# Long convolution and gated MLP on one core: stage-1 and last-stage tasks split into halves of one PSUM pair, with a new hand-written order

## The chip, the core and the metric

The kernel runs on one core of a Trainium2 chip. The core has a matrix engine (PE, with its weight loads shown apart as PEld), a vector engine (DVE), a scalar engine (ACT), a small general engine (POOL) and a queue engine (SP) that issues DMAs. They run at the same time and wait for one another through semaphores. The metric is the device time of one execution in microseconds (us); lower is better. Matmuls write into PSUM, eight banks of 128 x 512 fp32; only DVE and ACT read it.

## The reference

Input x (2048 x 512, called A_q) is layer-normalised to xn. Branch A shifts k by a 4-tap filter, multiplies it by v and convolves the product along the sequence with a filter of length 2048 per channel, by FFT. Branch B is a gated MLP on xn with 1792 hidden columns. The result joins them:

```python
kv = k_shift * v
y  = irfft(rfft(pad(kv)) * rfft(pad(ssm_k)))[:S] + kv * ssm_D
s  = xn * y
h  = gelu(xn @ w_gate) * (xn @ w_up)
out = x + s * silu(h @ w_down)
```

All inputs and the output are bf16.

## The kernel before

**Branch A** replaces the FFT by a transform in two stages each way. In stage 1 the matrix F1 multiplies the filter's transposed rows (HTr; eight tasks called H0 to H7) and the product of k and v (V; eight tasks K0 to K7). A contraction is over 64 rows, so PE works as two 64-row tiles, and two matmuls run at once on the two halves of the partitions. One task is four matmuls of 512 columns and fills two PSUM pairs (a pair is two banks, 1024 columns). ACT or DVE copies each pair to SBUF (AST), for H an addition on DVE follows, and a DMA stores the result to a scratch tensor in HBM (ZH, ZK). Stage 2 loads it back and multiplies 32 x 32 tiles, 16 matmuls at once (L1029); the products of the spectra are taken on DVE; the inverse's first stage is again 32 x 32 tiles, goes through scratch ZI, and the inverse's last stage multiplies G1 in two 64-column tiles (L1274): eight results psy0 to psy7, one PSUM pair each, taken two to a task of eight matmuls.

**Branch B** goes over four groups of 512 rows. For each of 14 column blocks, `unit` makes a gate and an up product (four full-array matmuls each, L641), ACT takes the GELU out of PSUM (L1195) and DVE multiplies (L1204) into HT. `down` multiplies HT by Wd, 14 matmuls in three tasks (4, 5, 5) for each 128 rows.

**Layer norm** of the first rows: DVE's statistics (L848), a variance on ACT or DVE (L858, L859), a power on POOL (L861), the normalised tile (L870), four transposes on PE (L891), and a copy from PSUM to xnT (L632, L635).

**Start.** DVE zeroes a block (L696), and PE multiplies zeros twelve times to warm up. POOL makes index tables (two for F1, L671 and L672, and four for the other tables, L675 to L678). DVE multiplies the first two (L720), and the sines of ACT make F1 and the 32 x 32 tables. `m_turn` (four ACT operations, L753) prepares the inverse's tables, which two transposing DMAs bring into place.

**Order.** Each piece of work is a task. `SEQ` is a list, written out by hand, of all task numbers; a "b" takes the second of two engines a task may run on, DVE in place of ACT for most copies. The tasks are emitted in that order, so it fixes the order on every engine and queue: SP issues the loads and most stores, ACT issues the stores of ZH and ZI. Semaphore waits follow from the data, the SBUF slots and the PSUM banks. Slots and banks are given out while the list is walked: `Pool_.find` takes the one that a table of durations in the kernel says is free the longest. Gate, up and down products may hold four banks at a time (`NF_BANKS`); the pairs of branch A come from the same eight.

A run of neighbouring PE tasks that leave the full array for tiles, and return, is called an excursion below. Before, each stage-1 task and each last-stage task is an excursion by itself.

Of the kernel before, what the change touches and what calls it, by code (L numbers as in the profile page):

```python
# [413 lines left out]
def build_kernel(nc, A_q, A_k, A_v, A_shift_k, A_ssm_k, A_ssm_D, B_w_gate, B_w_up, B_w_down, out):  # L414
    with ExitStack() as es0:
# [524 lines left out]
        def stage1(x, u, Z):  # L940
# [3 lines left out]
            if x == "K":  # L944
                def halves(e):
                    for i in range(2):
                        for b in range(2):
                            k = slice(64 * b, 64 * b + 64)
                            trk.op("PE", lambda h, i=i, b=b, k=k: h.matmul(ps(psl(pp[i]), b), lhsT=F1[k, :], rhs=V[k, 2 * u + i, :], start=True, stop=True, tile_position=(64 * b, 0)),  # L949
                                   r=[R_F1, R_V[2 * u + i]], w=[R_ps[psl(pp[i])][b]], accum=True)  # L950
                s1_tasks[x].append(S.add([("PE", 2 * T_FWD)], halves, r=[bF1, bKV[u // 2]], w=pp, lat=150.0, mode=2))
            if x == "H":
# [8 lines left out]
                def rows(p):  # L961
                    return ps(psl(p)).rearrange("p (d r) -> p r d", r=2)
# [295 lines left out]
        for j in range(8):  # L1258
# [6 lines left out]
            if j % 2 == 0:  # L1265
                continue
# [94 lines left out]
```

## Time and profile before

| | us |
|---|---|
| runs: median of three | 192.35 |
| runs: lowest, highest | 191.08, 192.36 |
| the profiled execution | 191.04 |
| its span, first to last instruction | 189.24 |
| PE busy | 184.5 |
| DVE busy | 168.6 |
| ACT busy | 138.3 |

A line of the profile's timeline gives start, duration, engine, source line, operation, the tile written and the tile read, shapes, and the count of instructions merged; in brackets follows the idle time before it and who ended it. Names that end in q are an engine's queue, where it issues DMAs. Matmuls overlap in the array, so starts, not ends, tell their pace. A shape 64*128 is a 64-row tile, 128*64 a 64-column tile, 32*32 a small one.

### The profile page before, as it was taken

Reading aid. Unit: us, or ns where it says so; the run is one execution under the profiler, and the core shown is the slowest. Engines: PE = TensorE matmul, PEld = TensorE weight load, DVE = VectorE, ACT = ScalarE, POOL = GpSimd, SP = SyncE. Lnnn points to the kernel's source line nnn. Section 1 sums busy time; section 2 is a strip of 40 time slices with the busy share of each in tenths; the row PEclk is TensorE's granted clock in tenths of the full one; section 3 lists DMA queues with packets and bytes.
Section 4 is the critical chain, followed back from the end, with each engine's and each line's share of the span. In section 5 each row is a group of like instructions: output and inputs, shape, how many; then the busy total and the mean of one; then the engine's idle time right before and its main releaser. Section 6 shows DMA issues by size and latency. Waiting matters only on the chain.

```text
span 189.2 us, 3611 instructions
## 1 busy us (share of the span) xinstructions
PE 184.5 (97%) x1418; PEld 79.6 (42%) x1418; DVE 168.6 (89%) x255; ACT 138.3 (73%) x191; POOL 11.1 (6%) x26
## 2 busy tenths in 40 slices
PE   7899999999999999999999999999999999999993
PEld 2685453333333333334444434333433344444342
DVE  5889999999999999988699999999999955458974
ACT  3789897988688786997548869688997672254671
POOL 5312600000000000022000000000000000000000
PEclk9999999999999999999999999999999999999999
DMA  5999999998769994468998966778742435946644
GB/s 173 329 384 344 345 373 367 400 416 326 210 254 249 362 227 161 171 215 229 324 261 214 321 221 182 291 259 276 273 156 74 149 128 157 366 143 182 256 178 166
DMA packets 36422, 47.84 MB, mean 253 GB/s; under 512 B 7347, under 2 KB 26039, under 8 KB 36406
## 3 DMA queue, kind: packets, MB, share of 16 engines
q1 hardware_dynamic: 29878, 39.23, 64.2%
q10 hardware_dynamic: 6528, 8.39, 12.6%
q8 instruction: 11, 0.18, 0.4%
q14 instruction: 5, 0.04, 0.1%
HBM read 27.39 MB, written 14.68 MB: 222 GB/s over the span
## 4 chain that ended last, share of the span: by engine, by line
PE 97%; DVE 1%; ACT 0%; issue 0%
PE psall L641 82%; PE psall L1029 6%; PE psall L957 2%; PE psall L949 2%; PE psall L915 2%; PE psall L1274 2%; PE psall L891 1%; DVE G L1239 0%; DVE G L1238 0%; ACT G L1236 0%; DVE xnT L635 0%; DVE AST L696 0%; DVE COLS L695 0%
## 5 line engine op out<-in xcount | busy, mean ns | idle before, releaser
L641 PE MATMUL psall<-xnT,Wu 128*128 128x512 bf16 (+1 forms) x248 | 56.3, 359 | 0.0
L641 PE MATMUL psall<-xnT,Wg 128*128 128x512 bf16 (+1 forms) x248 | 55.8, 359 | 0.5 <-DVE xnT L635 0.5
L641 PE MATMUL psall<-Wd,HT 128*128 128x512 bf16 (+2 forms) x238 | 52.3, 367 | 0.0
L1195 ACT ACTIVATE GE<-psall 128x512 bf16<-128x512 f32 x54 | 31.6, 602 | 12.2 <-PE psall L641 10.9
L641 PEld LDWEIGHTS psall<-Wd,HT 128*128 128x128 bf16 x238 | 21.7, 98 | 27.6 <-issue 4.8
L641 PEld LDWEIGHTS psall<-xnT,Wu 128*128 128x128 bf16 x248 | 22.0, 98 | 26.4 <-issue 2.6
L641 PEld LDWEIGHTS psall<-xnT,Wg 128*128 128x128 bf16 x248 | 21.5, 98 | 27.4 <-issue 3.3
L1204 DVE TENSOR_TENSOR HT<-psall,GE 128x512 bf16<-128x512 f32 x43 | 28.8, 682 | 3.0 <-PE psall L641 2.9
L632 ACT ACTIVATE BO<-psall 128x1024 bf16<-128x1024 f32 x20 | 20.0, 1026 | 7.9 <-PE psall L1274 6.0
L1132 DVE TENSOR_TENSOR HSW<-KB,HSW 128x2048 bf16<-128x2048 bf16 x16 | 19.1, 1216 | 0.1
L632 ACT ACTIVATE HSW<-psall 128x1024 bf16<-128x1024 f32 x15 | 14.7, 1026 | 4.7 <-PE psall L1029 4.6
L632 ACT ACTIVATE KB<-psall 128x1024 bf16<-128x1024 f32 x13 | 13.2, 1039 | 2.4 <-PE psall L1029 2.4
L1012 DVE TENSOR_TENSOR KAC<-KAC,KTM 128x2048 bf16<-128x2048 bf16 x12 | 14.6, 1217 | 0.1
L1010 DVE TENSOR_TENSOR KTM<-KK,SKB 128x2048 bf16<-128x2048 bf16 x12 | 14.6, 1216 | 0.0
L632 ACT ACTIVATE AST<-psall 128x1024 bf16<-128x1024 f32 x12 | 12.3, 1026 | 2.4 <-PE psall L641 2.0
L1228 ACT ACTIVATE G<-psall 128x512 bf16<-128x512 f32 x12 | 7.1, 601 | 7.3 <-PE psall L641 7.3
L632 ACT ACTIVATE XN<-psall 128x1024 bf16<-128x1024 f32 x10 | 10.3, 1029 | 0.8 <-PE psall L957 0.8
L1230 DVE SCALAR_TENSOR_TENSOR G<-G,psall 128x512 bf16<-128x512 bf16 x12 | 7.8, 679 | 3.2 <-ACT G L1228 3.2
L848 DVE BATCH_NORM_STATS2 stats<-X 128x6 f32<-128x512 bf16 x16 | 10.6, 676 | 0.0
L861 POOL TENSOR_TENSOR mv<-mv,NHALF 128x1 f32<-128x1 f32 (+1 forms) x7 | 5.5, 784 | 76.4 <-DVE mv L859 71.9
L1132 DVE TENSOR_TENSOR KB<-KB,HSW 128x2048 bf16<-128x2048 bf16 x8 | 9.6, 1216 | 0.0
L1155 DVE TENSOR_TENSOR HSW<-HSW 128x2048 bf16<-128x2048 bf16 x8 | 9.6, 1215 | 0.0
(89 smaller groups left out, 165.8 us busy)
## 6 DMA issues: line engine op xcount, KB each, us to landing
BH<-ZH SPq DMA_DIRECT2D x8, 512.0 KB, 4.8
BK<-ZK SPq DMA_DIRECT2D x8, 512.0 KB, 5.3
HSW<-HSW SPq DMA_DIRECT2D x16, 256.0 KB, 4.1
ZI<-BO ACTq DMA_DIRECT2D x16, 256.0 KB, 3.1
BI<-ZI SPq DMA_DIRECT2D x8, 512.0 KB, 4.9
ZK<-AST SPq DMA_DIRECT2D x6, 512.0 KB, 3.3
ZH<-XN ACTq DMA_DIRECT2D x5, 512.0 KB, 3.3
Hn<-in_A_ssm_k_dram SPq DMA_DIRECT2D x4, 512.0 KB, 7.3
```

Source lines behind the costliest of these rows:

```text
L632: return h.activation(o, i, ACTF.Copy, scale=scale)
L641: return h.matmul(o, lhsT=l, rhs=r, start=st, stop=sp)
L848: t_stats[t] = op([("DVE", 670.0)], lambda e, h, t=t: h.bn_stats(stats[:, t, :], X[:, t, :]), r=[bX[q][t % 4]], w=[bst[t]], rr=[R_X[t]], w ...
L1010: op([("DVE", dur)], lambda e, h, j=j, m=m: h.tensor_tensor(KTM[:, m.slot, :, :], kk(j), sk(j), ALU.mult), r=need + [bSKB[j], a], w=[m], r ...
L1012: op([("DVE", dur)], lambda e, h, m=m: h.tensor_tensor(KAC[:, a.slot, :, :], KAC[:, a.slot, :, :], KTM[:, m.slot, :, :], ALU.add), r=[m], ...
L1029: trk.op("PE", lambda h: h.matmul(ps(s, i)[b, :], lhsT=wt(col)[a, :], rhs=data(col)[a, :], start=n < 16, stop=n >= len(todo) - 16, tile_po ...
L1132: return hd.tensor_tensor(pair(KB, *(2 * DM * z for z in slots())) if to else x, k, x, ALU.mult)
L1155: return hd.tensor_tensor(x, x, y, ALU.add)
L1195: op([("ACT", act(512))], lambda e, h: h.activation(GE[:, g.slot, :], bank(pg), ACTF.Gelu_apprx_tanh), r=[pg], w=[g], rr=lambda: R_bank(pg ...
L1204: op([("DVE", dve(512, 1))], lambda e, h: h.tensor_tensor(HT[:, q % 2, m, :], bank(pu), GE[:, g.slot, :], ALU.mult), r=[pu, g], w=[bHT[q][m]],
L1228: op([("ACT", act(n))], lambda e, h, g=g, pc=pc: h.activation(g, pc(), ACTF.Tanh, scale=0.5), r=[p], w=[bt], rr=lambda p=p: R_bank(p), ww= ...
L1230: op([("DVE", dve(512, 1))], lambda e, h, g=g, pc=pc: h.scalar_tensor_tensor(out=g, in0=g, scalar=1.0, in1=pc(), op0=ALU.add, op1=ALU.mult ...
```

## The change

Stage-1 tasks are split. Before, one task filled two pairs; for H each 512-column half of the input was spread over both pairs, one partition half to each. Now there are two tasks for each of H0 to H7 and K0 to K7; task i takes the i-th half of the columns (H) or the i-th row block (K), and writes one pair, a partition half to each of its two banks. For H the copy of pair i, 1024 elements as before, fills half of the columns in each of AST's four rows (runs of 256), where it filled two whole rows, and task i waits only for the transposed blocks of its own columns. The last stage's four tasks of two results become eight of one. There are 816 tasks in place of 796, and as many instructions on PE.

The list is new throughout. In it up to three of the new tasks stand side by side:

```text
before  stage 1: 16 excursions of one task (four matmuls)
        last:     4 excursions of one task (eight matmuls)
after   stage 1: 13 excursions, of 1 to 3 tasks (two matmuls each)
          H3_0 H2_0 H1_0 | H7_0 H1_1 H2_1 | H3_1 | H5_0 H7_1 | H5_1 H6_1 H6_0
          H4_0 H0_0 H0_1 | H4_1 K1_0 K1_1 | K0_1 K0_0 K3_0 | K3_1 K2_0 K2_1
          K5_1 K5_0 | K4_1 K4_0 | K7_0 K7_1 | K6_0 K6_1
        last:     3 excursions, of 2 or 3 tasks (four matmuls each)
          psy2 psy0 | psy4 psy3 psy1 | psy7 psy5 psy6
```

At the start, POOL now makes the two index tables for F1 ahead of the other four, and DVE multiplies them ahead of the zeros. ACT takes the sines, and with them a table load, ahead of the first two variances. `m_turn` moves from the first GELUs to behind the copies of H6. Both late loads of x come ahead of the stage-2 loads of ZH on SP.

```diff
-    "3 16 0 1 17 18 2 7 19 20 21 22 23 24 25 26 4 27 10 8 11 67 68 28 65 5 9 66 73 29 6 48 49 30 76b 77 78 87 12 74 75 69 91 86 90b 361 70 349 350 31 "
+    "2 16 17 18 19 20 21 7 0 22 10 23 24 25 3 4 5 26 6 8 11 9 12 27 28 29 1 65 66 67 68 73b 74 75 76b 77 78 48 86 90 49 30 87 91 31 69 70 79 80 32 "
...
             if x == "K":
-                def halves(e):
-                    for i in range(2):
+                for i in range(2):
+                    def halves(e, i=i):
                         for b in range(2):
                             k = slice(64 * b, 64 * b + 64)
...
-                s1_tasks[x].append(S.add([("PE", 2 * T_FWD)], halves, r=[bF1, bKV[u // 2]], w=pp, lat=150.0, mode=2))
+                    s1_tasks[x].append(S.add([("PE", T_FWD)], halves, r=[bF1, bKV[u // 2]], w=[pp[i]], lat=150.0, mode=2))
             if x == "H":
-                def pairs(e):
-                    for i in range(2):
+                bl = B(f"low{u}")
+                for i in range(2):
+                    def pairs(e, i=i):
                         for b in range(2):
                             k = slice(64 * b, 64 * b + 64)
-                            trk.op("PE", lambda h, i=i, b=b, k=k: h.matmul(ps(psl(pp[b]), i), lhsT=F1[k, :], rhs=HTr[k, u, 512 * i:512 * i + 512], start=True, stop=True, tile_position=(64 * b, 0)),
+                            trk.op("PE", lambda h, b=b, k=k: h.matmul(ps(psl(pp[i]), b), lhsT=F1[k, :], rhs=HTr[k, u, 512 * i:512 * i + 512], start=True, stop=True, tile_position=(64 * b, 0)),
...
+                    s1_tasks[x].append(S.add([("PE", T_FWD)], pairs, r=[bF1] + [bHTr[k][u // 4] for k in range(2 * i, 2 * i + 2)] + ([bFold] if u == 0 else []), w=[pp[i]], lat=150.0, mode=2))
+                for i in range(2):
+                    op(EV(1024), lambda e, h, i=i: copy(e, h, ast[x][a.slot][:, :, :, 256 * i:256 * i + 256], ps(psl(pp[i])).rearrange("p (b d r) -> p b r d", b=2, r=2)), r=[pp[i]], w=[a, bl],
...
-                op(EV(1024), lambda e, h: copy(e, h, ast[x][a.slot][:, 0, :, :], rows(pp[0])), r=[pp[0]], w=[a, bl], rr=lambda: R_ps[psl(pp[0])], ww=lambda: [R_AST[x][a.slot]])
-                op(EV(1024), lambda e, h: copy(e, h, ast[x][a.slot][:, 1, :, :], rows(pp[1])), r=[pp[1]], w=[a, bl], rr=lambda: R_ps[psl(pp[1])], ww=lambda: [R_AST[x][a.slot]])
...
-            if j % 2 == 0:
-                continue

             def y(e, j=j):
-                for jj in (j - 1, j):
-                    s, slot = psl(p_y[jj]), b_bi[jj].slot
-                    for i in range(2):
-                        for b in range(2):
...
-            S.add([("PE", 4 * T_FWD)], y, r=[bG1, *b_bi[j - 1:j + 1]], w=p_y[j - 1:j + 1], lat=150.0, mode=3)
+            S.add([("PE", 2 * T_FWD)], y, r=[bG1, b_bi[j]], w=[p_y[j]], lat=150.0, mode=3)
```

More of the change, by code (lines that the diff above doesn't have):

```diff
@@ L944, in stage1 @@
             if x == "K":
-                def halves(e):
-                    for i in range(2):
+                for i in range(2):
+                    def halves(e, i=i):
                         for b in range(2):
                             k = slice(64 * b, 64 * b + 64)
-                            trk.op("PE", lambda h, i=i, b=b, k=k: h.matmul(ps(psl(pp[i]), b), lhsT=F1[k, :], rhs=V[k, 2 * u + i, :], start=True, stop=True, tile_position=(64 * b, 0)),
+                            trk.op("PE", lambda h, b=b, k=k: h.matmul(ps(psl(pp[i]), b), lhsT=F1[k, :], rhs=V[k, 2 * u + i, :], start=True, stop=True, tile_position=(64 * b, 0)),
@@ L955, in pairs @@
                         for b in range(2):
                             k = slice(64 * b, 64 * b + 64)
-                            trk.op("PE", lambda h, i=i, b=b, k=k: h.matmul(ps(psl(pp[b]), i), lhsT=F1[k, :], rhs=HTr[k, u, 512 * i:512 * i + 512], start=True, stop=True, tile_position=(64 * b, 0)),
-                                   r=[R_F1, *R_HTr[u][2 * i:2 * i + 2]], w=[R_ps[psl(pp[b])][i]], accum=True)
-                s1_tasks[x].append(S.add([("PE", 2 * T_FWD)], pairs, r=[bF1] + [bHTr[k][u // 4] for k in range(KD)] + ([bFold] if u == 0 else []), w=pp, lat=150.0, mode=2))
@@ L961, in rows @@
[L961 to L965 removed]
+                            trk.op("PE", lambda h, b=b, k=k: h.matmul(ps(psl(pp[i]), b), lhsT=F1[k, :], rhs=HTr[k, u, 512 * i:512 * i + 512], start=True, stop=True, tile_position=(64 * b, 0)),
+                                   r=[R_F1, *R_HTr[u][2 * i:2 * i + 2]], w=[R_ps[psl(pp[i])][b]], accum=True)
@@ L1264, in build_kernel @@
             S.add([("SP", ISSUE)], ld, r=bZ["I"], w=[bi], nbytes=W_BI)
-            if j % 2 == 0:
-                continue
             def y(e, j=j):
-                for jj in (j - 1, j):
-                    s, slot = psl(p_y[jj]), b_bi[jj].slot
-                    for i in range(2):
-                        for b in range(2):
-                            c = slice(64 * b, 64 * b + 64)
-                            trk.op("PE", lambda h, i=i, b=b, c=c, s=s, slot=slot: h.matmul(ps(s, i)[c, :], lhsT=G1[:, c], rhs=BI[:, slot, 2 * b + i, :], start=True, stop=True, tile_position=(0, 64 * b)),
-                                   r=[R_G1, R_BI[slot]], w=[R_ps[s][i]], accum=True)
-            S.add([("PE", 4 * T_FWD)], y, r=[bG1, *b_bi[j - 1:j + 1]], w=p_y[j - 1:j + 1], lat=150.0, mode=3)
+                s, slot = psl(p_y[j]), b_bi[j].slot
+                for i in range(2):
+                    for b in range(2):
+                        c = slice(64 * b, 64 * b + 64)
+                        trk.op("PE", lambda h, i=i, b=b, c=c, s=s, slot=slot: h.matmul(ps(s, i)[c, :], lhsT=G1[:, c], rhs=BI[:, slot, 2 * b + i, :], start=True, stop=True, tile_position=(0, 64 * b)),
+                               r=[R_G1, R_BI[slot]], w=[R_ps[s][i]], accum=True)
+            S.add([("PE", 2 * T_FWD)], y, r=[bG1, b_bi[j]], w=[p_y[j]], lat=150.0, mode=3)
         for j in range(8):
```

2 lines of the change are left out of this document (1 added, 1 removed), and 43 rows, old and new, of the table SEQ.

## The prediction

> **What bounds the kernel now.** I read the page first, then the list of waits of PE, then the busy time by stage.
>
> ```profile
> span 189.2 us, 3611 instructions
> PE 184.5 (97%) x1418; PEld 79.6 (42%) x1418; DVE 168.6 (89%) x255; ACT 138.3 (73%) x191; POOL 11.1 (6%) x26
> PE 97%; DVE 1%; ACT 0%; issue 0%
> ```
> ```profile
> PE psall L641 <- DVE AST L696: 1.2, 1, 1.2
> PE psall L641 <- DVE xnT L635: 0.5, 1, 0.5
> ```
> ```profile
> 9.00:45.00 36.00, 36.00 (x247) 18.62 (x244) 34.97 (x59) 32.47 (x50) 5.03 (x7) 1.00 1.04 371
> 45.00:80.00 35.00, 35.00 (x173) 13.38 (x172) 34.79 (x45) 27.47 (x37) 0.00 (x0) 1.00 0.77 244
> ```
>
> The chain of waits is PE for 97% of the span, and the only waits that PE shows are 1.2 us at the start (for the zeros that the warm-up multiplies) and 0.5 us (for the first transposed xn). In the columns of the two stages (window, length, PE, PE weight loads, DVE, ACT, POOL, clock, DMA, GB/s) PE is busy all 71 us, and DVE is hardly less full: 34.97 of 36 and 34.79 of 35. So a microsecond comes off only where PE itself does less, and a wait of PE, which had none here, shows at once. The number of matmuls is the same before and after, 1418. What can shrink is the time between them where PE changes its array shape.
>
> **The excursions.** The matmuls of stage 1 (64-row tiles, L949 and L957) and of the last inverse stage (64-column tiles, L1274) stand between full-array ones. PE's timeline around one of each:
>
> ```profile
> 50.73 1.03 PE L641 MATMUL psall<-xnT,Wu 128*128 128x512 bf16 x4
> 51.69 0.61 PE L949 MATMUL psall<-V,F 64*128 64x512 bf16 x4
> 52.23 1.25 PE L641 MATMUL psall<-Wd,HT 128*128 128x512 bf16 x5
> ```
> ```profile
> 170.68 1.03 PE L641 MATMUL psall<-xnT,Wu 128*128 128x512 bf16 x4
> 171.63 1.05 PE L1274 MATMUL psall<-BI,G 128*64 128x512 bf16 x8
> 172.62 0.60 PE L641 MATMUL psall<-Wd,HT 128*128 128x512 bf16 x2
> ```
> ```profile
> 84.60 0.43 PE L1029 MATMUL psall<-BH,TF 32*32 32x512 bf16 x16
> 84.97 3.84 PE L641 MATMUL psall<-Wd,HT 128*128 128x512 bf16 x17
> 88.74 0.43 PE L1029 MATMUL psall<-BH,TF 32*32 32x512 bf16 x16
> 89.11 3.19 PE L641 MATMUL psall<-Wd,HT 128*128 128x512 bf16 x14
> 92.23 0.43 PE L1029 MATMUL psall<-BK,TF 32*32 32x512 bf16 x16
> ```
>
> Starts are to be read, since ends are modelled. From 84.97 to 88.74 pass 3.77 us for 17 matmuls and one change of shape, from 89.11 to 92.23 pass 3.12 for 14 and one change: three matmuls are 0.65, one is 0.216, and the change takes 0.10. Into the 64-row excursion: four matmuls and the change in 0.96, so 0.10. Out of it: its four matmuls run two at a time, 0.43, and 0.54 pass, so 0.11. The 64-column one: 0.95 for four in front (0.09), and 0.99 for four steps of 0.216 behind (0.13). An excursion costs about 0.20 us beyond its matmuls, whatever it holds.
>
> Counting runs of tasks with the same shape in the two lists: before, 16 excursions in stage 1, 4 in the last stage and 24 of 32x32 tiles; after, 13, 3 and 24. The four that go are worth 4 x 0.20 = **0.8 us**. The splitting of tasks adds no matmul: each old task of four becomes two of two, each pair still runs at once, into two banks.
>
> On this price the Trainium skill differs: its page "TensorE: Matmul & The Clock Gate", section "Single matmul latency", puts an unhidden drain at about 175 ns. As an estimate by that page eight changes fewer would be 1.4 us, and the sum below would end 0.6 us lower. The trace's 0.09 to 0.13 decides.
>
> **What the new order moves: the start.** The new lists put POOL's two index tables (L671, L672) first and DVE's product of them (L720) ahead of the zeros (L696), for which the warm-up waits.
>
> ```profile
> 0.82 0.19 POOL L675 IOTA ARR<- 128x64 int32 x1 [0.39 <-POOLq L1346]
> 1.85 0.13 POOL L671 IOTA Q<- 128x1 int32 x1
> 1.93 0.18 POOL L672 IOTA K<- 128x64 int32 x1
> ```
> ```profile
> 0.79 0.06 DVE L695 MEMSET COLS<- 128x1 f32 x1 [0.79 <-PEq L1346]
> 0.88 0.27 DVE L696 MEMSET AST<- 128x256 uint32 x1
> 2.15 0.59 DVE L720 TENSOR_SCALAR C<-K,Q 128x64 int32<-128x64 int32 x2 [1.00 <-POOL K L672]
> ```
> ```profile
> 1.21 5.30 PE L641 MATMUL psall<-AST 128*128 128x512 bf16 x12 [1.21 <-DVE AST L696]
> 6.30 1.28 PE L915 MATMUL psall<-ident,Hn 128*128 128x128 f32 x8
> 7.42 0.61 PE L891 MATMUL psall<-ident,XN 128*128 128x128 bf16 x8
> 7.84 0.60 ACT L632 ACTIVATE xnT<-psall 128x512 bf16<-128x512 bf16 x1 [0.40 <-PE psall L891]
> 8.55 1.07 PE L641 MATMUL psall<-xnT,Wg 128*128 128x128 bf16 x16 [0.52 <-DVE xnT L635]
> ```
> ```profile
> 11.29 0.66 PE L915 MATMUL psall<-ident,Hn 128*128 128x128 f32 x4
> 11.78 0.61 PE L641 MATMUL psall<-xnT,Wg 128*128 128x128 bf16 x8
> ```
> ```profile
> 5.95 1.28 ACT L748 ACT_TABLE_LOAD   x1
> ```
>
> POOL begins at 0.82, the two tables took 0.26 (1.85 to 2.11): done at 1.08. DVE's product began 0.04 behind them and took 0.59: 1.12 to 1.71. The two memsets span 0.36 (0.79 to 1.15): zeros at 2.07, and PE follows 0.06 later, at 2.13 for 1.21. The warm-up took 5.09 (1.21 to 6.30): 7.22. Then four fp32 transposes of h, 0.49 (11.29 to 11.78): 7.71. Now come the first tile's xn transposes; ACT began its copy 0.42 behind such a start (7.42 to 7.84), takes 0.60, PE follows 0.06 later: first gate matmuls at 8.79. The second tile's transposes stand behind another four of h and are 0.71 later, at 8.42; their copy runs from 8.84 to 9.44, PE goes on at 9.50. Between, PE has eight small matmuls, 16 of which took 0.90 (8.55 to 9.45): 0.45, so it is done at 9.24. At 9.50 eight are done, and before that point was reached at 9.00: **0.5 us later**. This eats part of the wait for xn that PE had, but not all. From below: if the last warm-up matmul runs at the full rate (twelve took 5.09, or 0.42 each, while the eight transposes at 6.30 already speed up), 0.2 less; a gain is excluded, since no matmul can precede the zeros. From above: ACT's table load of 1.28 now stands ahead of both variance operations of the first tiles; with the phase arithmetic 0.6 earlier I estimate its end at 5.6 and the first normalised tile at 7.1, where PE wants it at 7.71. If that 0.6 of cover is gone, what exceeds it is added, up to 0.5.
>
> **The loads and queues.** The list of loads on SP is unchanged. Behind them, SP takes both late x loads ahead of the ZH loads for stage 2, whose readers on PE stand near 84.60, some 15 us behind their landing; and the swap of hs0 goes behind the transposing DMA that it preceded:
>
> ```profile
> 88.61 4.81 SPq L883 DMA_TRANSPOSE xnT<-XN  x1
> ```
> ```profile
> HSW<-HSW SPq DMA_DIRECT2D x16, 256.0 KB, 4.1
> ```
> ```profile
> 107.28 0.65 PE L1029 MATMUL psall<-KB,MI 32*32 32x512 bf16 x32
> ```
>
> So the swap is issued some 5 us later, near 93, and lands near 97; two DVE products of 1.2 us stand between it and PE's task at 107.28. It costs nothing, with 7 us to spare. One cover is thin, that of the first load of ZK:
>
> ```profile
> 80.01 0.36 SPq L614 DMA_DIRECT2D ZK<-AST  x1
> 84.48 0.91 SPq L614 DMA_DIRECT2D BK<-ZK  x2
> ```
> ```profile
> DMA to landing us min/median/max: 4.6/5.3/6.4
> ```
>
> It is issued when the last ZK store has landed (84.48) and needs 5.3: 89.8, and PE asks at 92.23, 2.4 us later. In the new order that task moves up: 22 down matmuls stand between the first stage-2 task of ZH and it, where 31 and another excursion stood, 9 x 0.216 + 0.41 = 2.35 us less. So the cover is used up to 0.1. By the shortest landing (4.6) it costs nothing, by the longest (6.4) 1.0 us. I take nothing, as the first of the two loads is the one wanted, and keep 0 to 1.0.
>
> DVE, nearly full to 80 us, has as much to do ahead of the last product of V as before or less (103 tasks for 106), so PE's earlier K tasks find their inputs. Vector and scalar work else is the same: the evacuation of stage 1's H tasks keeps 1024 elements per instruction, only reordered, and I cost that at nothing; should the shorter runs cost, ACT's slack of 3.5 us in the first stage window pays.
>
> **Sum.** The profiled execution took 191.04 us, of which 189.24 span. 191.04 - 0.8 + 0.5 + 0 = **190.7 us**. The four executions before lie at two levels, 191.04 and 191.08, 192.35 and 192.36; their median of 192.35 is 1.3 above the profiled one, and I know no reason in the profile. The same 0.3 off gives 190.7 or 192.0, and I forecast the middle, **191.4 us**.
>
> **Rivals.**
> (a) The start is hidden: the warm-up's end turns out not to bind, and the whole 0.8 comes off, 190.2 at the lower level. For it: PE already waits 0.5 us there. Against: the chain above is PE's own.
> (b) PSUM does not empty fast enough, and the change is slower. Nine of the new excursions hold three tasks; each fills three pairs, six of the eight banks; the seven in stage 1 do so in 3 x 0.216 + 0.2 = 0.85 us.
>
> ```profile
> L632 ACT ACTIVATE AST<-psall 128x1024 bf16<-128x1024 f32 x12 | 12.3, 1026 | 2.4 <-PE psall L641 2.0
> L1195 ACT ACTIVATE GE<-psall 128x512 bf16<-128x512 f32 x54 | 31.6, 602 | 12.2 <-PE psall L641 10.9
> ```
>
> A pair takes ACT 1.03 us to copy, so three take 3.1, and one GELU of 0.60 each 1.7 us of gate and up matmuls (eight of 0.216) comes on top. In the first stage ACT is 90% busy and in both DVE is 97% or more, so a copy that is late has nobody to take it. PE then waits at the third task, or at the next gate task. At 0.5 us in each of the nine it is 4.5 us, 195.2 on the profiled level; at 0.03 each the gain of 0.3 is gone, and from 0.24 each (2.2 us in all) it is slower by over 1%. Against it: the same copies were kept up with before, and the longer stretches of full-array matmuls between excursions give them as much time in the mean. The Trainium skill speaks for it ("TensorEngine Tiling (Array Packing)", section "PSUM Bottleneck": tiling speeds up PE but not the emptying of PSUM, which may become the bound); the trace before shows no PE wait of that kind.
> (c) The price of a change of shape sits with each task and not with each excursion, so merging saves nothing: 191.04 + 0.5 = 191.5 on the profiled level. Against it: the eight-matmul excursion of two tasks' worth cost 0.22 in all, as much as that of four.
>
> **Chances and range.** Forecast 0.52, (a) 0.14, (b) 0.24, (c) 0.10. One per cent, about what a measurement of this kernel can tell from no change, is 1.9 us. The forecast, (a) and (c) lie within it, but two levels 0.7% apart can carry (a) and a little of the forecast beyond it: faster 0.06. Of (b) I give half to waits over 0.24 us each, and the ZK load adds a little: slower 0.14. Same 0.80. The range goes from 190.0, (a) with part of the start's wait gone, to 193.4, the upper level with the ZK load's 1.0 on top; that leaves out the worse half of (b) and little else.
>
> **What would show it.** Stage 1 and last-stage matmuls in groups of four to six (L957, L949) and eight to twelve (L1274), with 0.2 us beyond their matmuls for each group; the first warm-up matmul at 2.1 and the gate matmuls at 8.8 with a second wait of 0.3 behind them. A wait of PE for ACT or DVE ahead of a three-task excursion speaks for (b), one for a DMA at the first BK task shows the lost cover. If the warm-up starts at 1.2 as before, my reading of the start is wrong; if PE's waits beyond the start sum to over 1 us, the forecast is.

## The result, and the profile after

| | before | after |
|---|---|---|
| median of 20 runs each, us | 191.89 | 191.16 |
| lowest to highest, us | 191.07 to 192.9 | 190.65 to 192.1 |
| ratio of the two, 95% interval | | 0.9963 (0.9945 to 0.9981) |
| the profiled execution, us | 191.04 | 190.82 |
| its span, us | 189.24 | 189.03 |

The kernel became 0.4% faster, by less than the one per cent that the prediction called "no change", and the interval lies below 1. The forecast was 191.4 us, and 190.7 for the profiled execution, which took 190.82: both times are close. The fall is less so. It was forecast as 0.3 us; the profiled pair fell by 0.22, the medians by 0.73. And how the 0.22 came about is not what the prediction said, as the trace shows.

From the page of after, the busy times and the shares of the chain of waits by engine:

```profile
PE 183.0 (97%) x1418; PEld 80.1 (42%) x1418; DVE 167.3 (88%) x252; ACT 140.2 (74%) x194; POOL 11.0 (6%) x26
...
PE 82%; DVE 7%; DMA 6%; issue 1%; ACT 1%; POOL 1%; SPq 0%; POOLq 0%
```

The list of PE's waits of after:

```profile
PE psall L642 <- DVE Q L727: 2.0, 1, 2.0
PE psall L892 <- DVE XN L871: 0.6, 1, 0.6
```

The chain was PE for 97% of the span before. Now 7% of it runs over DVE and 6% over a DMA, and PE waits for a normalised tile, which it did not before. The DMA is the load of k; it landed at 22.57, 0.85 us before DVE began the first product that reads it (23.42), and neither PE's list of waits nor DVE's names it. The busy time of after in the first of the two stages that were shown of before:

```profile
9.00:45.00 36.00, 35.18 (x239) 18.22 (x237) 35.02 (x58) 31.00 (x49) 4.57 (x7) 1.00 1.02 364
```

PE is busy 35.18 of the first 36 us, where it was busy all 36. The price of an excursion is as forecast. PE's timeline of after around a three-task excursion of stage 1, and around one of the last stage (each row begins with start and duration):

```profile
36.61 1.03 PE L642 MATMUL psall<-xnT,Wg 128*128 128x512 bf16 x4
37.57 0.82 PE L959 MATMUL psall<-HTr,F 64*128 64x512 bf16 x6
38.32 1.04 PE L642 MATMUL psall<-xnT,Wu 128*128 128x512 bf16 x4
...
171.66 1.49 PE L1270 MATMUL psall<-BI,G 128*64 128x512 bf16 x12
173.08 1.25 PE L642 MATMUL psall<-Wd,HT 128*128 128x512 bf16 x5
```

Into the first, 0.96 for four matmuls of 0.216 (0.10 extra). Out of it, 0.75 for three pairs (0.10). Out of the second, 1.42 for six steps of 0.216 (0.12). So about 0.2 for three tasks, as before for one or two. The merging did take 4 x 0.2 us off PE's own work, but most of it is not in the time of this execution. Three waits between 20 and 32 us, in PE's timeline of after:

```profile
20.71 1.03 PE L642 MATMUL psall<-xnT,Wu 128*128 128x512 bf16 x4
22.31 0.40 PE L892 MATMUL psall<-ident,XN 128*128 128x128 bf16 x4 [0.57 <-DVE XN L871]
...
25.86 2.20 PE L642 MATMUL psall<-xnT,Wg 128*128 128x512 bf16 x8
27.90 1.89 PE L642 MATMUL psall<-xnT,Wu 128*128 128x512 bf16 x8
...
30.58 0.90 PE L959 MATMUL psall<-HTr,F 64*128 64x512 bf16 x4
31.42 1.04 PE L642 MATMUL psall<-xnT,Wg 128*128 128x512 bf16 x4
```

From 20.71 to 22.31 are 1.60 us for four matmuls (0.86): 0.74 lost, for the sixth normalised tile. From 25.86 to 27.90, 2.04 for eight (1.73): 0.31 lost, for a PSUM bank. The two-task excursion at 30.58 takes 0.84 where two pairs and the way out take 0.54: 0.30 lost inside it, for a bank again. Together 1.35 us. In each case the releaser is a DVE instruction. PE's list of waits shows only 0.6 of this; the rest is seen in the starts alone. PE's timeline of before, where the first transposes of those tiles came at 23.33:

```profile
23.33 0.61 PE L891 MATMUL psall<-ident,XN 128*128 128x128 bf16 x8
...
24.59 0.74 PE L957 MATMUL psall<-HTr,F 64*128 64x512 bf16 x4
25.27 0.40 PE L891 MATMUL psall<-ident,XN 128*128 128x128 bf16 x4
```

There PE did not wait for them. It was not quite without losses, though: from 24.59 to 25.27 are 0.68 for two pairs and the way out (0.54), and three more of 0.08 to 0.10 stand at 19.7, 22.5 and 57.7 us, 0.4 in all. DVE's timeline of after at the time of the first wait:

```profile
19.27 0.69 DVE L1203 TENSOR_TENSOR HT<-psall,GE 128x512 bf16<-128x512 f32 x1
19.87 1.17 DVE L930 TENSOR_TENSOR HTr<-HTr,Drow 1x512 bf16<-1x512 bf16 x1
20.95 0.59 DVE L866 SCALAR_TENSOR_TENSOR NB__69<-mv 128x4 f32<-128x4 f32 x1
21.57 1.32 DVE L871 TENSOR_SCALAR XN<-X,mv 128x512 bf16<-128x512 bf16 x3
```

and POOL's of after:

```profile
19.22 2.88 POOL L986 COPY SKB<-SKR 128x512 bf16<-128x512 bf16 x4 [0.70 <-DMA SKR<-in_A_shift_k_dram]
```

DVE has no gap here. It adds one row of 512 elements in 1.17 us and a tile of 128 x 4 in 0.59, while POOL copies. The start, in PE's timeline of after:

```profile
2.01 4.36 PE L642 MATMUL psall<-AST 128*128 128x512 bf16 x12 [2.01 <-DVE Q L727]
6.20 0.60 PE L916 MATMUL psall<-ident,Hn 128*128 128x128 f32 x4
...
8.08 1.25 PE L642 MATMUL psall<-xnT,Wg 128*128 128x128 bf16 x16
...
11.50 0.39 PE L642 MATMUL psall<-xnT,Wg 128*128 128x128 bf16 x4
```

The warm-up begins at 2.01, as forecast (2.13), but its twelve matmuls take 4.19 us for 5.09. At the gate product that came at 11.78 before, PE is 0.28 us earlier and not 0.5 later. What all this comes to is read where DVE's last product of V (the input of stage 1's K tasks) meets PE. DVE's timeline of before, then PE's of before, then the same of after:

```profile
73.48 1.23 DVE L1014 TENSOR_TENSOR V<-KAC,V 128x2048 bf16<-128x2048 bf16 x1
```
```profile
75.07 0.61 PE L949 MATMUL psall<-V,F 64*128 64x512 bf16 x4
```
```profile
73.59 1.23 DVE L1013 TENSOR_TENSOR V<-KAC,V 128x2048 bf16<-128x2048 bf16 x1
```
```profile
75.10 0.61 PE L950 MATMUL psall<-V,F 64*128 64x512 bf16 x4
```

75.07 and 75.10: at that task nothing has been gained, though the same matmuls and three excursions fewer lie ahead of it. On the way the start gave -0.28, the three excursions -0.6, the small losses of before -0.4 and the three waits +1.35: +0.07, where +0.03 is measured. From there to the end of the span are 114.17 us before (189.24 - 75.07) and 113.93 after, 0.24 less, and 0.2 of that is the one excursion fewer in the last stage.

### The profile page after: what moved, and what is told of

It is laid out like the page before. It is cut to its first block, busy times and chain, and to the rows that moved or that the text cites. A ratio compares the mean times of both kernels' runs of the same rounds, so it can differ in the third digit from the quotient of the medians.

```text
span 189.0 us, 3595 instructions
## 1 busy us (share of the span) xinstructions
PE 183.0 (97%) x1418; PEld 80.1 (42%) x1418; DVE 167.3 (88%) x252; ACT 140.2 (74%) x194; POOL 11.0 (6%) x26
## 4 chain that ended last, share of the span: by engine, by line
PE 82%; DVE 7%; DMA 6%; issue 1%; ACT 1%; POOL 1%; SPq 0%; POOLq 0%
PE psall L642 71%; DMA KK<-in_A_k_dram 6%; PE psall L1028 6%; PE psall L950 2%; PE psall L1270 2%; PE psall L959 1%; DVE KTM L1009 1%; DVE HT L1203 1%; ACT L749 1%; DVE XN L965 1%; DVE stats L849 1%; DVE KAC L1005 1%; DVE KAC L1011 1%; POOL mv L862 1%; DVE XN L871 1%
## 5 line engine op out<-in xcount | busy, mean ns | idle before, releaser
L642 PE MATMUL psall<-xnT,Wg 128*128 128x512 bf16 (+1 forms) x248 | 56.5, 359 | 0.2
L642 PE MATMUL psall<-xnT,Wu 128*128 128x512 bf16 (+1 forms) x248 | 55.7, 359 | 0.0
L642 PEld LDWEIGHTS psall<-xnT,Wu 128*128 128x128 bf16 x248 | 22.5, 98 | 25.5 <-issue 1.7
L633 ACT ACTIVATE BO<-psall 128x1024 bf16<-128x1024 f32 x19 | 18.9, 1023 | 9.2 <-PE psall L1270 5.5
L633 ACT ACTIVATE HSW<-psall 128x1024 bf16<-128x1024 f32 x16 | 15.7, 1023 | 3.1 <-PE psall L1028 2.2
L633 ACT ACTIVATE KB<-psall 128x1024 bf16<-128x1024 f32 x14 | 13.9, 1027 | 2.6 <-PE psall L1028 2.4
L633 ACT ACTIVATE AST<-psall 128x1024 bf16<-128x1024 f32 x10 | 10.2, 1023 | 1.4 <-PE psall L950 0.9
L633 ACT ACTIVATE X<-psall 128x1024 bf16<-128x1024 f32 x8 | 8.1, 1025 | 3.9 <-PE psall L959 3.9
```

Source lines behind the costliest of these rows:

```text
L633: return h.activation(o, i, ACTF.Copy, scale=scale)
L642: return h.matmul(o, lhsT=l, rhs=r, start=st, stop=sp)
```

## The experiments

Ratios are to the kernel before on the same chip. There were four chips, with medians of 191.58 to 191.78 us for the kernel before; the change itself, run again on one of them, had 190.99 us. Numbers in the short diffs of the list are task numbers: 64 is DVE's 1 x 512 addition ("fold"), 404, 392, 413 and 440 are HT products.

My theory after the traces was D: in the changed kernel DVE sets the pace between 14 and 31 us, slowed by POOL's copies, and hides there what PE saves. Against it stood that the price of an excursion is not what it seemed (B, C), that the order alone makes DVE late (E), and that a cost taken from DVE only moves (F). Theory H, which came later, is told where it arose.

**The changed kernel again.** No edit.

> The changed kernel itself, for comparison on the same chip with the three below. Ratio to the kernel before 0.996 (0.994 to 0.998), about 0.8 us less. In the trace three waits of PE on DVE between 21 and 31 us of together 1.3 us, as in the first trace, and DVE's addition on 1 x 512 (L930) again near 1.2 us, if this comes from the instructions beside it and not from chance; if it was chance, both differ.

Measured: 190.99 us, ratio 0.9961 (0.9935 to 0.9987). Its profiled execution took 190.82 us as well, with a later start. PE's timeline of this execution:

```profile
2.01 5.08 PE L642 MATMUL psall<-AST 128*128 128x512 bf16 x12 [2.01 <-DVE Q L727]
6.92 0.60 PE L916 MATMUL psall<-ident,Hn 128*128 128x128 f32 x4
...
8.44 1.34 PE L642 MATMUL psall<-xnT,Wg 128*128 128x128 bf16 x16
...
21.17 1.03 PE L642 MATMUL psall<-xnT,Wu 128*128 128x512 bf16 x4
22.31 0.40 PE L892 MATMUL psall<-ident,XN 128*128 128x128 bf16 x4
```

The gate product is 0.36 us later than in the first trace (8.44 for 8.08), the products ahead of the wait 0.46 (21.17 for 20.71), and the tile's transposes begin at 22.31 in both: the wait has shrunk from 0.74 to 0.28, and every later task starts at the same time as in the first trace. So between these two executions the start makes no difference to the time. The expected sum of the waits (1.3) was wrong for that reason, and the addition took 0.98 us, less than in the first trace (1.17) and than expected, but more than the 0.75 of before.

**Three-task excursions split.**

```diff
   96 129
-  95
   153 442
+  95
   529 97
...
   231 233
+  446
   232 234
-  446
   457 247
...
```

(Two of eight such moves: 95 and 232 are third tasks, 442 and 446 full-array ones.)

> The changed kernel with eight of its nine three-task excursions split: the third task goes behind the next full-array task, so there are 48 excursions for 40. Theory A (each excursion costs about 0.19 us beyond its matmuls, and PE sets the pace after 31 us): 7 of the 8 lie after 31 us, 7 x 0.19 = 1.3 us more than the changed kernel, up to 1.5 if the one near 19 us is not hidden; ratio to it 1.007 to 1.008. Theory B (three tasks in a row wait for PSUM to be emptied): the split takes such waits away, 0 to 0.5 us net more or even less. Theory C (the price sits with each task, not with each excursion): no difference.

Measured: 193.62 us, ratio 1.0089 (1.0059 to 1.0119), 2.6 us more than the changed kernel. PE's timeline around one third task (68.12) and the next excursions:

```profile
67.78 0.38 PE L642 MATMUL psall<-Wd,HT 128*128 128x512 bf16 x1
68.12 0.39 PE L950 MATMUL psall<-V,F 64*128 64x512 bf16 x2
68.44 1.25 PE L642 MATMUL psall<-Wd,HT 128*128 128x512 bf16 x5
69.63 0.91 PE L950 MATMUL psall<-V,F 64*128 64x512 bf16 x4
...
71.69 0.39 PE L950 MATMUL psall<-V,F 64*128 64x512 bf16 x2
72.74 0.39 PE L950 MATMUL psall<-V,F 64*128 64x512 bf16 x2 [0.67 <-ACT AST L633]
```

The split task costs 0.34 - 0.216 on the way in and 0.32 - 0.216 on the way out: 0.23. Two splits lie before 31 us, not one as I wrote, and six behind. PE is 0.52 us later than in the trace of after at 31 us and 2.82 at 75 us (77.92 for 75.10), with five splits between. Two waits are in it, 0.30 (0.91 for 0.61 at 69.63) and 0.83 (72.74 - 71.69 - 0.216), so five splits cost 1.17 us, 0.23 each, and the sixth adds 0.23 near 184 us. The price of an excursion is shown, and theory C has fallen. Theory B has fallen in the sense meant, since splitting takes no wait away. The two new waits are of its kind, though: tasks for which ACT has not emptied a pair (1.03 us each). Why the split makes them was not followed up. Together 1.13 us, they are about what the expectation was short by (2.6 for 1.3 to 1.5).

**POOL's copies later.**

```diff
         skb = [op([("POOL", 650.0)],
...
-  rr=[R_SKR]
+  rr=[R_SKR, R_XN[7]]
...
-  144
+  143
   476 390 113 480
+  144
   145
-  143
   147 392
```

(142 to 145 are the four copies; now they run in the order in which they are read.)

> The changed kernel with POOL's four copies of the shift coefficients held back until DVE has normalised the eighth tile of x, and in the order in which DVE reads them. Theory D (DVE sets the pace from 14 to 31 us, and POOL's copies slow the DVE operations beside them): the 1 x 512 addition takes 0.4 to 0.75 us for 1.18, the small tile behind it 0.2 to 0.3 for 0.59, the normalised tile 0.40 for 0.68; PE's waits from 21 to 31 us shrink from 1.3 us to 0.5 or less, and the time falls by 0.5 to 1.2 us against the changed kernel (ratio to the kernel before 0.990 to 0.994). Rival E (POOL's copies have nothing to do with it, the order alone makes DVE late): durations and waits stay, ratio to the changed kernel 1.000. Rival F (the cost moves on): the 128 x 2048 products, 1.21 us now, take its place and get 0.3 to 0.6 longer each, the waits stay near 1.3 us or move past 27 us, no gain.

Measured: 191.31 us, ratio 0.9987 (0.9961 to 1.0012). DVE's timeline of this kernel, then POOL's:

```profile
20.63 0.71 DVE L930 TENSOR_TENSOR HTr<-HTr,Drow 1x512 bf16<-1x512 bf16 x1
21.24 0.14 DVE L866 SCALAR_TENSOR_TENSOR NB__69<-mv 128x4 f32<-128x4 f32 x1
21.42 1.06 DVE L871 TENSOR_SCALAR XN<-X,mv 128x512 bf16<-128x512 bf16 x3
...
23.62 1.64 DVE L1005 TENSOR_TENSOR KAC<-KK,SKB 128x2048 bf16<-128x2048 bf16 x1 [0.54 <-POOL SKB L986]
```
```profile
22.55 3.81 POOL L986 COPY SKB<-SKR 128x512 bf16<-128x512 bf16 x4 [3.27 <-DVE XN L871]
```

Half of theory D is shown: without a copy beside them, the three kinds of DVE instruction take 0.71 for 1.17, 0.14 for 0.59 and 1.06 for 1.32 (three tiles), 1.17 us less in all. Rival E, that the copies have nothing to do with it, has fallen. But rival F holds for the time: the first product for the shift waits 0.54 for its copy and then takes 1.64 for 1.21, the second waits 0.53 for the next copy, and PE waits there (1.03 us near 27). The four copies take 3.81 us in place of 2.88. Eight of the twelve runs lie within 0.02 us of 191.30. The profiled execution took 192.06 and is not one of them, so its trace need not show what decides there.

**Zeros first again.**

```diff
+  0
   2 16
...
-  0
   22 10
```

> The changed kernel with DVE's two memsets back in first place, ahead of the product of the index tables, as before the change. The warm-up begins near 1.2 us for 2.0, the sines and F1 up to 0.36 us later. Forecast's theory (the warm-up's start binds PE): 0.5 us less than the changed kernel, ratio 0.997. Theory D (DVE sets the pace to 31 us, an earlier PE only waits longer there): PE reaches its gate products earlier by up to 0.5 us, the waits from 21 to 31 us grow by as much, ratio 0.999 to 1.001. Third case (the later F1 now binds the first transposes or stage 1): up to 0.4 us more.

Measured: 190.89 us, ratio 0.9958 (0.9934 to 0.9982), as the changed kernel (0.9961). The time is theory D's case, but the trace is not: in the profiled execution (191.76 us) the warm-up began at 1.21, PE then waited 0.83 us for the load of the gate weights, and its gate products began at 8.78, later than in both traces of after. The 0.5 us that the forecast charged for the zeros is not in the median; whether DVE or that load hides it stays open.

**The fold later on DVE.**

```diff
   58 62
-  64
   136 138
...
   155 418
+  64
   131 127
```

> The changed kernel with one DVE instruction moved: the 1 x 512 addition (L930), whose result PE first reads near 43 us, goes from 20 us to near 38 us, out of the stretch in which POOL copies. Theory D (DVE sets the pace from 14 to 31 us): the sixth normalised tile is ready 0.7 to 1.2 us earlier, PE's three waits between 21 and 31 us shrink from 1.3 us to 0.1 to 0.6, PE passes 31 us that much earlier and keeps it: 0.7 to 1.2 us less than the changed kernel, near 190.1, ratio to the kernel before 0.990 to 0.993. Rival F (the cost moves on): the tiles behind it meet POOL's copies in its place, gain 0 to 0.3 us. Rival G (something behind 31 us takes the gain back, a DMA or the later place of the addition): PE is earlier at 31 us but the end stays, ratio to the changed kernel 1.000.

Measured: 190.70 us, ratio 0.9947 (0.9928 to 0.9966), 0.3 us less than the changed kernel (their intervals overlap), 0.4 to 0.9 short of what theory D expected. PE's timeline near 44 us:

```profile
43.16 1.25 PE L642 MATMUL psall<-Wd,HT 128*128 128x512 bf16 x5
44.61 1.04 PE L642 MATMUL psall<-xnT,Wg 128*128 128x512 bf16 x4 [0.20 <-DVE HT L1203]
```

In this execution PE was 0.64 us later at the start, 0.34 earlier at 27 us, and then lost 0.37 here (1.45 for five matmuls, 1.08). So DVE holds PE not only to 31 but to 44 us. That led to theory H, in which the sum of DVE's work counts: the moved addition still takes 0.72 us at 38, so only some 0.5 us is really saved.

**HT products first.** As the last, and:

```diff
   391 110
+  404
   146
-  404
...
+  392
   147
-  392
...
-  116
   411 413
+  116
```

> As the kernel with the addition moved, and besides three pieces of DVE work that nobody wants soon (two products for the shift, one addition on a stage-1 result, 0.7 to 1.2 us each) go behind the HT product that they preceded between 22 and 30 us, so that PSUM banks come free earlier. Theory D: the waits that are left at the gate product near 27 us (0.30) and in the excursion near 31 us (0.29) go too; against the kernel with the addition moved alone 0 to 0.4 us less, and PE shows no wait over 0.1 us between 21 and 31 us. Rival: DVE then waits for PE's products at those places, and the shift products are late at the first V tasks near 51 us: equal or up to 0.5 us more.

Measured: 191.00 us, ratio 0.9972 (0.9947 to 0.9996), no better than without it. In the profiled execution PE is 1.17 us earlier than in the trace of after at 31 us. It loses 0.35 of that inside a three-task excursion, and 0.57 near 44 us. PE's timeline:

```profile
36.42 1.17 PE L959 MATMUL psall<-HTr,F 64*128 64x512 bf16 x6
```

1.17 for the 0.82 of the row above at 37.57: the last matmul starts right behind the end of one of DVE's HT products (37.15). Putting DVE's work in another order gained PE time here that it lost at the next place where it needed DVE.

**The start alone, in the kernel before.**

```diff
+  2
   3 16
+  17 18 7
   0 1
-  17 18 2 7
```

> The kernel before with the start's new order on POOL and DVE alone (index tables for F1 first, their product ahead of the memsets; ACT's order stays as before). Forecast's term: warm-up from 2.1 us for 1.2, first gate products at 8.8 for 8.55, 0.5 us later with the second wait, and PE has no wait behind it to hide that: ratio to the kernel before 1.0025, 0.2 to 0.7 us more. Theory D applied to before (DVE is full there as well, and PE has some slack behind it): 0 to 0.2 us more. Third case (the earlier sines help F1): up to 0.3 us less.

Measured: 191.59 us, ratio 0.9990 (0.9962 to 1.0018). The interval holds the 0.2 us of theory D and ends below the forecast's 0.5 (1.0026), though not below the lower part of its range. In the profiled execution the gate products begin at 8.93 for 8.55, and PE is 0.56 us later from 23 us to the end, so there a late start is carried on: 0.4 of it comes from the start, and 0.16 is lost near 23 us, where PE waits for an HT product of DVE. It is 191.61 us to the 191.04 of the profiled run before. The medians do not show it.

**The split code in the old order.** The split code, with the list of before in which the halves of each old task stand side by side. For H0, where 94 was the task and 95 its first copy (the numbers behind a split task move up):

```diff
-  94 95
+  94 95 96
```

> The split code with the order of the kernel before: the halves of each old task stand side by side, so there are 44 excursions as before, and the start is as before. Forecast's step (the split itself costs nothing, the gain is in the excursions): ratio to the kernel before 0.999 to 1.001. Theory C turned round (each task has a price of its own): 20 more tasks, at 0.1 us each 2 us more, ratio 1.010. If the copies in shorter runs or the earlier release of a pair matter, up to 0.5 us either way.

Measured: 191.65 us, ratio 1.0003 (0.9981 to 1.0026). The split itself costs and gains nothing, as forecast.

**The fold on POOL.**

```diff
-        h_fold = op([("DVE", 420.0)], lambda e, h: h.tensor_tensor(HT0, HT0, Drow[:], ALU.add),
+        h_fold = op([("POOL", 900.0)], lambda e, h: h.tensor_tensor(HT0, HT0, Drow[:], ALU.add),
...
   58 62
-  64
   136 138
...
   145 143
+  64
   147 392
```

> The changed kernel with the 1 x 512 addition (L930) moved from DVE to POOL, behind POOL's four copies. Theory H (what counts is the sum of DVE's work up to the last product of V near 75 us, not its order; PE passes the first task on that product 1.5 us behind the product's start in all traces so far): DVE is rid of 1.18 us near 20 us and loses perhaps 0.3 to 0.6 to POOL's addition beside it, the last product of V starts 0.6 to 0.9 us earlier than in the changed kernel (73.6), and the time falls by as much: near 190.3, ratio to the kernel before 0.991 to 0.994. Theory D in its first form (only PE's waits from 21 to 31 us count): 0.7 to 1.2 us less. Rival F (POOL's addition slows DVE by as much as it saves): as the changed kernel, 0.996.

Measured: 191.27 us, ratio 0.9990 (0.9963 to 1.0017). Rival F, and a little worse. DVE's timeline, then POOL's:

```profile
21.23 2.16 DVE L871 TENSOR_SCALAR XN<-X,mv 128x512 bf16<-128x512 bf16 x3
```
```profile
19.34 2.41 POOL L986 COPY SKB<-SKR 128x512 bf16<-128x512 bf16 x4
21.71 1.21 POOL L930 TENSOR_TENSOR HTr<-HTr,Drow 1x512 bf16<-1x512 bf16 x1
```

The three tiles take 2.16 us where they take 1.06 without POOL. Work given to POOL came back on DVE.

**The fold on two elements.** The list as with the fold later on DVE, and:

```diff
-        h_fold = op([("DVE", 420.0)], lambda e, h: h.tensor_tensor(HT0, HT0, Drow[:], ALU.add),
+        h_fold = op([("DVE", 420.0)], lambda e, h: h.tensor_tensor(HT0[:, 0:2], HT0[:, 0:2], Drow[:, 0:2], ALU.add),
```

510 of the 512 additions of ssm_D are left out.

> The kernel with the addition moved to 38 us, but on 2 of its 512 elements (the other 510 additions of ssm_D are left out). Theory H: DVE's sum is 0.5 to 0.6 us less than in the kernel with the whole addition there (0.72 us near 38 us), and 1.1 less than in the changed kernel; the wait of PE near 44 us (0.36 in that trace) goes, the last product of V starts near 72.6 for 73.6, 0.3 to 0.6 us less than with the whole addition, 189.9 to 190.4. Rival I (the place of the addition is what matters, not the sum): no difference from the kernel with the whole addition there, 190.7.

Measured: 190.55 us, ratio 0.9926 (0.9895 to 0.9957). DVE's timeline, then PE's:

```profile
72.83 1.23 DVE L1013 TENSOR_TENSOR V<-KAC,V 128x2048 bf16<-128x2048 bf16 x1
```
```profile
74.33 0.61 PE L950 MATMUL psall<-V,F 64*128 64x512 bf16 x4
```

The product of V starts 0.76 us earlier than in the trace of after (72.83 for 73.59), PE's task 0.77 earlier, and the span is 0.7 shorter (188.3). Against the kernel with the whole addition at the same place (73.63 and 75.13) it is 0.80. But of that 0.42 was there at 31 us (30.65 for 31.07), ahead of the instruction that was cut; 0.38 came behind it, and the wait near 44 (0.37) is gone. So less work on DVE takes away a wait that PE showed. That the sum counts, wherever the work stands, is not shown by it. In the medians the step from the whole addition is 0.15 us (190.70), short of the 0.3 to 0.6 expected; the ratios differ by 0.0021, inside their intervals, so rival I is not excluded either.

**The fold on POOL, in the kernel before.** The kernel before, with:

```diff
-        h_fold = op([("DVE", 420.0)], lambda e, h: h.tensor_tensor(HT0, HT0, Drow[:], ALU.add),
+        h_fold = op([("POOL", 900.0)], lambda e, h: h.tensor_tensor(HT0, HT0, Drow[:], ALU.add),
...
   106 61
-  64
   63b 386
...
   404 135
+  64
   139 398
```

> The kernel before with the same addition moved to POOL, and nothing else. There PE has no waits between 9 and 75 us and meets the last product of V 0.36 us after its end. Theory H: PE itself sets the pace there, DVE gains 0.3 to 0.7 us which nobody uses, ratio to the kernel before 0.999 to 1.001, and the distance between that product's end and PE's task grows from 0.36 to 0.7 us or more. Rival J (DVE set the pace in the kernel before as well, hidden in steady running): 0.3 to 0.7 us less, ratio 0.997.

Measured: 191.57 us, ratio 0.9997 (0.9971 to 1.0022). The time is H's, but the sign that was to come with it did not: the distance between the product and the task did not grow (74.35 to 75.93, less 1.23: 0.35). DVE gained nothing, since four tiles took 2.27 us beside POOL's addition, for 1.36. Between H and J this decides nothing.

**One shift addition behind an HT product.** The kernel with the fold near 38 us, and:

```diff
-  158
   424 426
...
   439 440
+  158
```

> The kernel with the addition moved to 38 us, and one addition of the shift (1.23 us) put behind the HT product that frees the bank for which PE waited 0.36 us near 44 us. Theory H (DVE's sum up to the last product of V bounds PE): the wait near 44 us goes, but DVE's sum is the same, so PE can keep only what the slack at that product allows (it starts its task 1.50 us behind the product's start, and 1.23 + 0.06 = 1.29 is the least): 0.2 us less than with the addition moved alone, a wait of PE on V near 75 us if it arrives with more than that, 190.4 to 190.6 us, ratio to the kernel before 0.992 to 0.995. Theory D in its first form (PE's shown waits are the cost): the whole 0.36 us comes off, 190.3, and the distance at the last product of V falls to 1.14, which would need V unfinished, or V is earlier. Rival: DVE waits for PE's up product in the new place, no gain.

Measured: 190.30 us, ratio 0.9940 (0.9909 to 0.9971), the lowest median of all kernels that do the whole work. Its interval overlaps that of the changed kernel, so that it beats it is not shown. The median alone is that of theory D's first form (190.3) rather than H's (190.4 to 190.6); the interval holds both. The profiled execution was one of the late ones (191.30; near 18 us PE waited 0.6 us for ACT's copy of transposed blocks). DVE's timeline, then PE's:

```profile
74.21 1.23 DVE L1013 TENSOR_TENSOR V<-KAC,V 128x2048 bf16<-128x2048 bf16 x1
```
```profile
74.50 1.03 PE L642 MATMUL psall<-xnT,Wu 128*128 128x512 bf16 x4
75.59 0.61 PE L950 MATMUL psall<-V,F 64*128 64x512 bf16 x4
```

The wait near 44 us is gone. From 74.50 four matmuls and the change take 0.96, so PE could have begun at 75.46, and it begins at 75.59, behind the end of V's product (75.44): 0.13 us is lost, as theory H said, at a distance of 1.38 and not 1.29. The profile names no releaser, so that V is the cause is read from the times alone. In the trace of after the distance is 1.51 (75.10 - 73.59). PE is thus within 0.13 us of waiting for DVE there. It is 1.50 or 1.51 in the eight traces of the new order other than this one and that of the split, and 1.58 to 1.60 in the four of the old order, whatever was moved: the two engines come to this place together. Which holds the other, the distance does not say.

## Why the prediction came out right

**What bounds the kernel.** The step "a microsecond comes off only where PE itself does less" failed as a sufficient reason. PE was busy all 71 us, and so was DVE, to 97% and 99%. PE shows no wait in such a stage when the other engine is just in time, and nothing in the list of waits says how close that is. By the distance at the last product of V it was 0.2 us (1.59 before, 1.38 at the least seen).

**The excursions, -0.8.** The price was right: 0.20 in the trace, 0.23 when eight were split. Where they lie decides the rest. Three of the four lie ahead of 75 us, where DVE sets the pace, and are not in the trace's time. The fourth, in the last stage, is. That DVE took the other three back is shown for the trace. How much of them comes into the median by other ways stays open (below).

**The start, +0.5.** The time of the zeros was right to 0.12 us, but the twelve matmuls took 4.19 for the 5.09 that I carried over, and in the second trace 4.91. More important, in the changed kernel a late start ends in a shorter wait at 22 us (0.45 us in the one trace became 0 in the other), and neither putting the zeros back nor the start alone in the kernel before moved a median beyond its interval. This was rival (a) in its mechanism, but not in its price, since the other term did not come off in full.

**DVE, 0.** The step that failed outright is "DVE, nearly full to 80 us, has as much to do ahead of the last product of V as before or less (103 tasks for 106), so PE's earlier K tasks find their inputs". The K tasks did find them. But a count over 80 us says nothing of who is asked when, and V is not all that PE needs from DVE: it needs the normalised tiles, and the PSUM banks that the HT products free. The new order asks for the sixth normalised tile near 21.6, when PE is through with the four matmuls that begin at 20.71. DVE, slowed by POOL's copies, had it at 22.3. The term that was put at 0 is 1.35 us in the first trace, 0.9 in the second. By the prediction's own sign, waits beyond the start of over 1 us, its account is wrong in the first trace. That the sum held all the same is luck: 1.35 cancelled the earlier start, the excursions ahead of 75 us and losses of before that the prediction had not seen; in the second trace 0.9 cancelled -0.6, -0.4 and a start that was 0.17 late (11.95 for 11.78).

**Loads, queues and evacuation, 0.** Right: no wait stands at the first BK task. Its cover was thinner than reckoned, since an excursion of 32 x 32 tiles is 0.47 by the rows (0.37 and 0.10) and not 0.41: 0.02 us was left, not 0.1. ACT's copies of H into runs of 256 took 1025 ns for 1028.

**The rivals.** (b), PSUM not emptied, cost none of the nine three-task excursions anything in the trace of after; the 0.30 us in a two-task one is a bank that DVE held. What the Trainium skill says may come of tiling ("TensorEngine Tiling (Array Packing)", section "PSUM Bottleneck": PE gets faster, the emptying of PSUM does not) shows here in that 0.30, in the 0.35 us where PE came a microsecond earlier (with the HT products first), and where the tasks were split. (c) fell with the split. The Trainium skill's figure for a drain ("TensorE: Matmul & The Clock Gate", section "Single matmul latency", about 175 ns) is not what a change of shape cost: 0.09 to 0.13 us in all of these rows.

**Trace and median.** The trace pair differs by 0.22 us, the medians by 0.73. The forecast of 191.4 rests on two levels that four executions of before seemed to show; the 20 of the table do not show them (nine lie between 191.2 and 192.2), so that the middle of the two came close to the median is luck too. Over the runs that were compared, 124 of before and 32 of after, a tenth lie below 191.07 and 190.65, half below 191.70 and 191.16, and nine tenths below 192.73 and 191.77. The spread has shrunk from 1.7 to 1.1 us. That fits a kernel in which late starts end in a shorter wait, where the one before carried them on (0.56 us to the end, with the start changed alone). This is argued from two pairs of traces and was not tested by itself, so the cause of the medians' 0.73 stays open.

## What to carry to other kernels

Where two engines are both full, take from the traces the distance between a product of the one and the task of the other that reads it: the distance less the least one seen bounds what the reader can gain there by itself as long as the other's times stay, and the list of waits doesn't show that. Read waits from the starts; the list had 0.6 of 1.35 us. A count of tasks over a long stage does not show that inputs are in time; follow the first task that is asked for earlier. Before work is given to an idle engine, look at what the neighbours' instructions beside it cost.

## What was unexpected of the hardware

**POOL beside DVE.** DVE's instructions with their data in SBUF took longer beside POOL's copies: the 1 x 512 addition up to 1.17 us for 0.71, the 128 x 4 tile up to 0.59 for 0.14, three normalised tiles up to 2.01 for 1.06 (2.16 where POOL's addition followed the copies), one 128 x 2048 product 1.64 for 1.21. By how much differs between executions (the addition took 0.75 in the trace of before, beside the same copies, and 1.10 with the split code in the old order). HT products, which read PSUM and one SBUF operand, took 0.69 in both cases. POOL paid as well: 2.41 to 3.81 us for the same four copies. The Trainium skill ("SBUF — State Buffer", section "Who interferes with whom") states that DVE and GpSimd (POOL) share a pair of ports, that an instruction with two SBUF inputs or in a two-port mode contends for it, the former with a GpSimd instruction that reads SBUF, and that one with a single SBUF input outside those modes does not. The rows agree: the addition and the product have two SBUF inputs, and HT has one. For the normalised tiles, with one SBUF tile and a scalar each, no row shows whether a two-port mode is in use.

**The first matmuls.** The pace of a 128 x 512 matmul goes from 0.43 to 0.216 us at a moment that differs between executions of one kernel: the twelve warm-up matmuls took 4.19 us in one trace of after and 4.91 in the other, both from 2.01, with the granted clock at 1.00 in both. The Trainium skill ("TensorE: Matmul & The Clock Gate", section "Part 1: The HAM clock gate (the "warmup" mystery)") explains such a change by a free-running window; the change of moment agrees, and no run here shows the window itself.
